# A gMLP block turned to have batch rows on lanes, and its output weight loaded as 72 lanes of 12 rows

## The chip, the core and the metric

The kernel runs on one core of a Trainium2 chip. The number that counts is the device time of one execution in microseconds (us). The kernel before takes 662.63 us, the median of three runs (662.47 to 662.69).

The core has five engines that matter here: TensorE (PE) multiplies, VectorE (DVE) and ScalarE (ACT) work on elements, GpSimd (POOL) sets up constants, and SyncE (SP) issues most of the transfers. Sixteen DMA engines carry data from HBM into SBUF, whose 128 partitions are called lanes below.

## The reference

One token for each of four batch rows goes through two branches that read the same normalised input, and their results are added to the input:

- x is 4 x 640; xn is its layer norm.
- Branch A is attention against a long cache: q = xn @ wq for 32 heads of 128; scores against 4096 cached keys for each row and head; softmax; the weighted sum of the cached values; then @ wo (4096 x 640). The two caches are 4 x 32 x 4096 x 128 in bf16 each, 134 MB each.
- Branch B is a gated MLP: z = gelu(xn @ w_in), with w_in 640 x 1728; z splits in two halves z1 and z2 of 864 columns; z2 is layer-normed over its 864 columns, multiplied by the single number w_sp and shifted by the single number b_sp; the product z1 * z2 goes through w_out (864 x 640).
- out = x + A + B.

Nearly all of the bytes are the caches: 282 MB are read in all, of which w_in is 2.2 MB and w_out 1.1 MB.

## The kernel before, in words

**Tiles.** The caches come in tiles of 128 lanes x 64 KB (8.4 MB): one tile holds one batch row's eight heads. There are 16 tiles of keys and 16 of values. Key tiles alternate between two buffers (the function `k_slot`); value tiles have a single buffer (`v_slot`). The two buffers of keys and the one of values are used for the weights first: `w_sb`, which sits in the buffer of the values, holds w_in (17,280 bytes in each lane) and behind it w_out; wq sits in one of the two key buffers.

**Order of the transfers.** SP issues all large transfers in the order of the program, and each of the 16 DMA engines takes its packets in that order: w_out's first part (L109), wq (L114), w_in (L121), w_out's rest (L123, four transfers), key tile 0 (L139, `load_k`), key tile 1 once wq has been read, value tile 0 (L145, `load_v`) once the gated MLP has read all of `w_sb`, key tile 2 once key tile 0 has been used up, and so on; wo comes last (L159, `load_wo`). A wait of SP for a buffer therefore stands in front of all transfers behind it.

**Order of the work.** The order on PE, DVE, ACT and SP is the program's (a manual schedule). After q, the first tile's query is spread over the lanes (`stage_q`), then comes `gmlp()`, then the loop over the tiles. For a tile, DVE multiplies keys by the query in two halves (L449), folds the product (L463), PE sums it (L475), DVE reduces the sums (L486) and the maxima, ACT takes the exponentials (L542), and PE weighs the values (L568). While tile i is multiplied, the values of tile i-1 are weighed. At the end wo's pieces are multiplied (`group_proj`, L216) as they land, and four small transfers write the result.

**The gated MLP before.** The 864 columns of a half lie as 128 x 6 and a rest of 96. Weights are the stationary side: for each half, seven groups of columns and five slices of the 640 inputs there is one matmul with 4 columns, the batch rows (L317, 70 in all), so that features lie on lanes and the four batch rows along them: 128 lanes x 56 numbers. The gelu (L326 to L337) runs on tiles of that size. The sums of the layer norm run across lanes, so they take a matmul with a column of ones (L342), a few instructions on one lane (L351 to L378), and a matmul with a row of ones that spreads the two resulting factors again (L387). The gated product `yT` has features on lanes already. Its rest of 96 features is turned by six small matmuls to 16 lanes of six rows (L408), and 12 groups of four matmuls (`add_out`, L216) add the product with w_out to `out_ps`.

**w_out before.** The first 768 rows go to 128 lanes with six rows, 7,680 bytes, each (L109). The last 96 rows go to lanes 0 to 15, six rows each, in four transfers of four lanes (L123); transfer l of them fills the lanes l, l+4, l+8 and l+12.

Of the kernel before, what the change touches and what calls it, by code (L numbers as in the profile page):

```python
# [17 lines left out]
def kernel(  # L18
# [35 lines left out]
    SLOT = NC * Dh  # L54
    CB = 4
    NB = NC // CB
    CG = 4
    GW = P // CG
# [5 lines left out]
    WJ = WH * Dh // P  # L64
    WW = 2
    WR = NG * ROWS
    NFF = Fh // P
    TL = 16
    TK = (Fh - NFF * P) // TL
    TE = 4  # L70
    NFC = NFF + TK
    F0 = NFF * P
    TF = TL * TK
    NZ = NFF + 1
    assert F0 + TF == Fh and TF <= P
    NQ = 4
    NO = D // NQ
    REP = GW // Bsz
# [5 lines left out]
    work = ctx.enter_context(tc.tile_pool(name="work", bufs=1))  # L84
# [12 lines left out]
    def v_slot(name):  # L97
# [7 lines left out]

    w_sb = v_slot("w_sb")
    w_in_sb = w_sb[:, 0 : DC * F].rearrange("p (c n) -> p c n", c=DC)
    w_out_sb = w_sb[:, DC * F : DC * F + NFC * D].rearrange("p (k n) -> p k n", k=NFC)
# [73 lines left out]
    for i in range(NSTAT):  # L182
# [9 lines left out]
        out=xn_bf,  # L192
# [21 lines left out]
    def add_out(lhsT, rhs, start=False, stop=False):  # L214
        for q in range(NQ):
            nc.tensor.matmul(  # L216
                out=out_ps[GW * q : GW * q + lhsT.shape[1], :],
                lhsT=lhsT,
                rhs=rhs[:, q * NO : (q + 1) * NO],
                start=start,  # L220
                stop=stop,
            )
# [36 lines left out]
    nc.gpsimd.tensor_copy(out=row_batch[:], in_=row_batch_f[:])  # L259


    HQ = 4
    NW = HQ * Dh
    q_rows = small.tile([P, 2, NW], BF16, tag="two_k", name="q_rows")
# [29 lines left out]
    load_k(1)  # L294


    GM = 2 * NZ * Bsz
    gm = {}
    gm_t = small.tile([P, 4 * GM + NZ * Bsz], FP32, tag="two_k", name="gm_t")
    for n, name in enumerate(("zz", "gw", "gt", "gz")):  # L300
        gm[name] = gm_t[:, n * GM : (n + 1) * GM].rearrange(
            "p (t k b) -> p t k b", t=2, b=Bsz
        )
    gm["sq"] = gm_t[:, 4 * GM :].rearrange("p (k b) -> p k b", b=Bsz)
    nc.gpsimd.memset(gm["zz"], 0.0)
    gm["st"] = work.tile([1, 5 * Bsz], FP32, name="st")
    gm["ac"] = work.tile([1, 2 * Bsz], FP32, name="ac")

    def gmlp():
        zz, gw, gt, gz, sq = (gm[n] for n in ("zz", "gw", "gt", "gz", "sq"))  # L310
        zT = ps_pv.tile([P, 2, NZ, Bsz], FP32, tag="pv", name="zT")
        for t in range(2):
            f1 = t * Fh + F0
            w_t = w_in_sb[:, :, t * Fh : f1].rearrange("p c (f k) -> p c k f", k=NFF)
            for k in range(NZ):
                for c in range(DC):
                    nc.tensor.matmul(  # L317
                        out=zT[: P if k < NFF else TF, t, k, :],
                        lhsT=w_t[:, c, k, :] if k < NFF else w_in_sb[:, c, f1 : f1 + TF],
                        rhs=xnT[:, c, :],  # L320
                        start=(c == 0),
                        stop=(c == DC - 1),
                    )
        nc.vector.tensor_copy(out=zz[:, :, 0:NFF, :], in_=zT[:, :, 0:NFF, :])
        nc.vector.tensor_copy(out=zz[:TF, :, NFF:NZ, :], in_=zT[:TF, :, NFF:NZ, :])
# [12 lines left out]
        nc.vector.tensor_tensor(out=sq, in0=gz[:, 1, :, :], in1=gz[:, 1, :, :], op=ALU.mult)  # L338

        s_ps = ps_m.tile([1, 2, NZ, Bsz], FP32, tag="m", name="ln_ps")  # L340
        for n, src in enumerate((gz[:, 1, :, :], sq)):
            nc.tensor.matmul(  # L342
                out=s_ps[:, n, :, :], lhsT=ones_col[:], rhs=src, start=True, stop=True
            )
        st, ac = gm["st"], gm["ac"]
        mean_t = st[:, 0:Bsz]
        ex2_t = st[:, Bsz : 2 * Bsz]
        var_t = st[:, 2 * Bsz : 3 * Bsz]
        rst_t = st[:, 3 * Bsz : 4 * Bsz]
        tmp_t = st[:, 4 * Bsz : 5 * Bsz]  # L350
        nc.vector.tensor_reduce(  # L351
            out=st[:, 0 : 2 * Bsz].rearrange("a (n b) -> a n b", b=Bsz),
            in_=s_ps[:].rearrange("a n k b -> a n b k"),
            axis=AX.X,
            op=ALU.add,
        )
        nc.vector.tensor_scalar(
            out=st[:, 0 : 2 * Bsz],
            in0=st[:, 0 : 2 * Bsz],
            scalar1=1.0 / float(Fh),  # L360
            scalar2=None,
            op0=ALU.mult,
        )
        nc.vector.tensor_tensor(out=tmp_t, in0=mean_t, in1=mean_t, op=ALU.mult)
        nc.vector.tensor_tensor(out=var_t, in0=ex2_t, in1=tmp_t, op=ALU.subtract)
        nc.scalar.activation(
            out=rst_t, in_=var_t, func=ACT.Sqrt, bias=eps_tile[:1], scale=1.0
        )
        wsp_t = work.tile([1, 1], FP32, name="wsp_t")
        nc.vector.tensor_copy(out=wsp_t[:], in_=wsp_bf[:])  # L370
        bsp_t = work.tile([1, 1], FP32, name="bsp_t")
        nc.vector.tensor_copy(out=bsp_t[:], in_=bsp_bf[:])
        nc.vector.reciprocal(out=rst_t, in_=rst_t)
        nc.vector.tensor_scalar(
            out=ac[:, 0:Bsz], in0=rst_t, scalar1=wsp_t[:, 0:1], scalar2=None, op0=ALU.mult
        )
        nc.vector.tensor_tensor(out=tmp_t, in0=ac[:, 0:Bsz], in1=mean_t, op=ALU.mult)
        nc.vector.tensor_scalar(  # L378
            out=ac[:, Bsz : 2 * Bsz],
            in0=tmp_t,  # L380
            scalar1=-1.0,
            scalar2=bsp_t[:, 0:1],
            op0=ALU.mult,
            op1=ALU.add,
        )
        ac_ps = ps_m.tile([P, 2 * Bsz], FP32, tag="m", name="ac_ps")
        nc.tensor.matmul(  # L387
            out=ac_ps[:], lhsT=ones_row[:], rhs=ac[:], start=True, stop=True
        )
        ac_sb = work.tile([P, 2 * Bsz], FP32, name="ac_sb")  # L390
        nc.scalar.copy(out=ac_sb[:], in_=ac_ps[:])
        nc.vector.tensor_tensor(
            out=sq,
            in0=gz[:, 1, :, :],
            in1=ac_sb[:, None, 0:Bsz].to_broadcast([P, NZ, Bsz]),
            op=ALU.mult,
        )
        nc.vector.tensor_tensor(
            out=sq,
            in0=sq,  # L400
            in1=ac_sb[:, None, Bsz : 2 * Bsz].to_broadcast([P, NZ, Bsz]),
            op=ALU.add,
        )
        yT = work.tile([P, NZ, Bsz], BF16, name="yT")
        nc.vector.tensor_tensor(out=yT[:], in0=gz[:, 0, :, :], in1=sq, op=ALU.mult)
        ye_ps = ps_m.tile([TL, TK, Bsz], FP32, tag="m", name="ye_ps")
        for k in range(TK):
            nc.tensor.matmul(  # L408
                out=ye_ps[:, k, :],
                lhsT=ident[:TF, :TF].rearrange("p (f k) -> p k f", k=TK)[:, k, :],  # L410
                rhs=yT[:TF, NFF, :],
                start=True,
                stop=True,
            )
        yE = work.tile([TL, TK, Bsz], BF16, name="yE")
        nc.scalar.copy(out=yE[:], in_=ye_ps[:])
        for k in range(NFC):
            if k < NFF:
                add_out(yT[:, k], w_out_sb[:, k, :])
            else:  # L420
                add_out(yE[:, k - NFF], w_out_sb[:TL, k, :])


    qbcs, scores, sums_ps, maxes, pms, pvs, es = {}, {}, {}, {}, {}, {}, {}
# [344 lines left out]
```

## Time and profile before

| what | value | where it is from |
|---|---|---|
| time, median of three runs | 662.63 us | timed runs |
| span of the profiled execution, first to last instruction | 661.1 us | page, head |
| around the span (start and end of the program) | 1.5 us | 662.63 less 661.1 |
| read from HBM | 282.24 MB, 427 GB/s over the span | page, part 3 |
| the large queue's share of the 16 DMA engines | 98.9% | page, part 3 |
| DVE busy | 491.6 us (74%) | page, part 1 |
| PE busy | 295.4 us (45%) | page, part 1 |
| gated MLP: first matmul to last | 23.85 to 35.64 us | timeline |
| DVE starts on key tile 0 | 43.24 us | timeline |
| last wo piece multiplied from | 657.27 us | timeline |

The page gives the profiled execution as one span, from its first instruction to its last, and that span is its own time; the timed runs are 1.5 us longer. In the views of transfers a window is cut into 40 slices, and a packet counts in the slice where it starts: one packet of 65,536 bytes in a slice of 0.1 us shows as 655 GB/s, one of 7,680 bytes as 77.

### The profile page before, as it was taken

The numbers are of one execution on the slowest core, as the hardware profiler recorded it, in microseconds if no ns is written. First come the engines' busy times: TensorE is split into PE (matmuls) and PEld (weight loads), VectorE is DVE, ScalarE is ACT, GpSimd is POOL, SyncE is SP. The second block draws the span as 40 slices with busy tenths as digits, with TensorE's granted clock in tenths as the row PEclk, the third lists the DMA queues.
The fourth block names the chain that finished last, engine by engine and source line by source line (L and its number), as shares of the span: only waits on it lengthen the run. The fifth ranks groups of instructions, "written<-read, shape, count | busy, mean of one in ns | idle before, by whom it ended". The sixth has DMA issues, their size and how long they took to land.

```text
span 661.1 us, 4720 instructions
## 1 busy us (share of the span) xinstructions
PE 295.4 (45%) x2099; PEld 127.9 (19%) x2099; DVE 491.6 (74%) x222; ACT 34.4 (5%) x94; POOL 2.1 (0%) x15
## 2 busy tenths in 40 slices
PE   0513464536426253552625344362634507263656
PEld 0301121212112021220202112120211202031223
DVE  1249999959597795959779569986959699695851
ACT  0300000000000000000000000000000000000000
POOL 1000000000000000000000000000000000000000
PEclk9756676876858687675868757787775768777688
DMA  8999999999999999999999999999999999999996
GB/s 377 456 428 444 428 417 441 429 436 441 436 420 433 432 429 445 440 421 432 424 436 441 440 425 432 420 441 436 437 428 437 425 432 429 440 432 437 432 406 275
DMA packets 5712, 282.55 MB, mean 427 GB/s; under 512 B 680, under 2 KB 812, under 8 KB 1084
## 3 DMA queue, kind: packets, MB, share of 16 engines
q1 hardware_dynamic: 5664, 282.24, 98.9%
q8 instruction: 16, 0.26, 0.2%
q14 instruction: 4, 0.03, 0.0%
q10 hardware_dynamic: 28, 0.01, 0.0%
HBM read 282.24 MB, written 0.01 MB: 427 GB/s over the span
## 4 chain that ended last, share of the span: by engine, by line
DMA 51%; DVE 37%; PE 9%; issue 2%; ACT 1%; SPq 0%; DVEq 0%; ACTq 0%
DMA k_nat<-in_A_k_cache_dram 47%; DVE k_nat L449 22%; DVE k_nat L463 11%; PE s_ps L475 8%; DMA wo<-in_A_wo_dram 4%; DVE s_sb L486 3%; DMA w_sb<-in_B_w_out_dram 1%; ACT p L542 1%; PE pv L568 1%; DVE m L495 1%; PE mT L500 0%; DVE nm L505 0%; DVE pm L553 0%; SPq L159 0%; PE out_ps L216 0%
## 5 line engine op out<-in xcount | busy, mean ns | idle before, releaser
L449 DVE TENSOR_TENSOR k_nat<-k_nat,qbc 128x16384 bf16<-128x16384 bf16 x32 | 278.0, 8688 | 97.8 <-DMA k_nat<-in_A_k_cache_dram 97.8
L475 PE MATMUL s_ps<-k_nat,ident 128*128 128x512 bf16 x528 | 184.8, 528 | 139.3 <-DVE k_nat L463 139.3
L463 DVE TENSOR_TENSOR k_nat<-k_nat 128x8192 bf16<-128x8192 bf16 x31 | 136.7, 4410 | 0.0
L475 PEld LDWEIGHTS <-ident 128*128 128x128 bf16 x528 | 65.3, 129 | 248.3 <-DVE k_nat L463 123.3
L500 PE MATMUL mT<-ident_f,m 128*1 128x128 f32 x16 | 5.9, 366 | 160.0 <-DVE m L495 160.0
L568 PE MATMUL pv<-v_nat,pm 128*32 128x512 bf16 x960 | 56.1, 387 | 0.8 <-DVE pm L553 0.8
L486 DVE TENSOR_REDUCE s_sb<-s_ps 128x128 f32<-128x1024 f32 x32 | 39.0, 1218 | 5.4 <-PE s_ps L475 5.4
L500 PEld LDWEIGHTS mT<-ident_f,m 128*1 128x1 f32 x16 | 1.3, 79 | 167.8 <-DVE m L495 156.2
L568 PEld LDWEIGHTS <-pm 128*32 128x32 bf16 x1024 | 27.1, 100 | 34.3 <-issue 8.5
L553 DVE TENSOR_TENSOR pm<-p,own_c 128x2048 bf16<-128x2048 bf16 x16 | 19.6, 1225 | 15.3 <-ACT p L542 15.3
L542 ACT ACTIVATE p<-s_sb,nb 128x256 bf16<-128x256 f32 x16 | 8.1, 508 | 394.1 <-DVE nb_h L524 394.1
L591 PE MATMUL o_ps<-e,pick 128*32 128x128 f32 x128 | 17.0, 276 | 11.2 <-ACT e L578 11.2
L591 PEld LDWEIGHTS o_ps<-e,pick 128*32 128x32 f32 x128 | 12.7, 109 | 18.7 <-ACT e L578 18.7
L578 ACT COPY e<-pv 128x512 f32<-128x512 f32 x16 | 9.4, 586 | 68.1 <-PE pv L568 60.6
L287 DVE COPY qT<-qT_ps 128x64 bf16<-128x64 bf16 x2 | 0.4, 224 | 15.5 <-PE qT_ps L282 15.5
L516 PE MATMUL nb_ps<-nm,ones_row 1*128 1x8 f32 x32 | 9.2, 359 | 6.0 <-DVE nm L505 6.0
L505 DVE TENSOR_REDUCE nm<-mT 1x8 f32<-1x128 f32 x16 | 4.5, 279 | 7.5 <-PE mT L500 7.5
L516 PEld LDWEIGHTS nb_ps<-nm,ones_row 1*128 1x128 f32 x32 | 7.7, 298 | 10.6 <-DVE nm L505 9.9
L271 PE MATMUL q_ps<-wq,xnT_r 128*32 128x512 bf16 x40 | 4.3, 609 | 11.2 <-DMA wq<-in_A_wq_dram 11.2
L443 ACT CAST qbc<-qbc_ps 128x128 bf16<-128x128 f32 x16 | 4.3, 266 | 92.3 <-PE qbc_ps L435 92.3
L608 PE MATMUL den<-ones_col,acc_h 128*32 128x1 f32 x8 | 1.0, 194 | 16.6 <-DVE acc_h L601 16.6
L495 DVE TENSOR_REDUCE m<-s_sb 128x1 f32<-128x256 f32 x16 | 6.7, 420 | 0.5
(92 smaller groups left out, 70.7 us busy)
## 6 DMA issues: line engine op xcount, KB each, us to landing
wq<-in_A_wq_dram SPq DMA_DIRECT2D x1, 5120.0 KB, 16.3
wo<-in_A_wo_dram SPq DMA_DIRECT2D x1, 2560.0 KB
w_sb<-in_B_w_in_dram SPq DMA_DIRECT2D x1, 2160.0 KB, 20.9
wo<-in_A_wo_dram SPq DMA_DIRECT2D x1, 1760.0 KB
w_sb<-in_B_w_out_dram SPq DMA_DIRECT2D x1, 960.0 KB
wo<-in_A_wo_dram SPq DMA_DIRECT2D x1, 640.0 KB, 25.5
k_nat<-in_A_k_cache_dram SPq DMA_DIRECT2D x16, 39.6
v_nat<-in_A_v_cache_dram SPq DMA_DIRECT2D x15, 33.7
```

The source lines that it names most:

```text
L449: nc.vector.tensor_tensor(out=part(i, u), in0=part(i, u), in1=qbcs[i][:, None, :].to_broadcast([P, UC, Dh]), op=ALU.mult,)
L463: nc.vector.tensor_tensor(out=t[:, :, 0:HD2], in0=t[:, :, 0:HD2], in1=t[:, :, HD2:Dh], op=ALU.add)
L475: nc.tensor.matmul(out=sums_ps[i][:, c : c + SC], lhsT=ident[:], rhs=t[:, c : c + SC, g * RW : (g + 1) * RW], start=(g == 0), stop=(g == n ...
L486: nc.vector.tensor_reduce(out=scores[i][:, u * UC : (u + 1) * UC], in_=sums_ps[i][:], axis=AX.X, op=ALU.add,)
L495: nc.vector.tensor_reduce(out=m1[:], in_=scores[i][:], axis=AX.X, op=ALU.max)
L500: nc.tensor.transpose(out=mT[:], in_=maxes[i][:], identity=ident_f[:])
L516: nc.tensor.matmul(out=nb_ps[:], lhsT=ones_row[:], rhs=maxes[i][:], start=True, stop=True)
L542: nc.scalar.activation(out=probs[i][:], in_=scores.pop(i)[:], func=ACT.Exp, bias=maxes.pop(i)[:], scale=scale_qk, accum_out=accs[hg][:, b ...
L553: nc.vector.tensor_tensor(out=pm[:], in0=probs.pop(i)[:] .rearrange("p (n c) -> p n c", c=CB)[:, :, None, :] .to_broadcast([P, NB, HT, CB] ...
L568: nc.tensor.matmul(out=pvs[i][j * GW : (j + 1) * GW, :], lhsT=pm[:, n, :, :].rearrange("p h c -> p (h c)"), rhs=v_nat[:, n * CB : (n + 1) ...
L578: nc.scalar.copy(out=es[i][:], in_=pvs.pop(i)[:].rearrange("p (c d) -> p c d", d=Dh))
L591: nc.tensor.matmul(out=o_ps[hg // NG][own_rows(hg), :], lhsT=pick[:, c, GW - HT - HT * b : 2 * GW - HT - HT * b], rhs=e[:, c, :], start=(b ...
```

## The change

The gated MLP is computed with the batch rows as the stationary side, and w_out is laid out anew.

- 20 matmuls of 32 x 432 (each of five input slices by four groups of lanes) replace the 70. The stationary side is xn with each batch row repeated eight times, as for q. Lanes 32j to 32j+31 hold the features of group j, three of every twelve columns; the result is 128 lanes x 432 numbers (both halves), every batch row eight times over.
- The gelu and the gate run on 128 x 432 and 128 x 216. The layer norm's sums run along a lane (two reductions) and then over the four groups with one matmul against a new constant, `same_row`, made of the identity matrix by one DVE reduction and one GpSimd copy. The factors then lie on every lane; the spreading matmul with its copy goes, and a small matmul spreads w_sp and b_sp.
- The gated product is turned by three transposes into 72 lanes, and 12 groups of `add_out` follow, with 72 lanes each.
- The working tiles and `same_row` now lie behind the weights in `w_sb`; a GpSimd memset and a tile of the small pool go.
- w_out goes to 72 lanes of 12 rows (15,360 bytes each): lanes 0 to 47 in one transfer ahead of wq, lanes 48 to 53, 54 to 59, 60 to 65 and 66 to 71 in four transfers behind w_in.

The number of transfers, their order and their 1,080 KB for w_out stay. Value tile 0 still goes into the buffer of `w_sb` when all of its readers are done.

```diff
+    FL = 72
+    FK = Fh // FL
+    FM = FK // CG
+    FC = Fh // CG
+    F_CUTS = (0, 48, 54, 60, 66, FL)
...
-    nc.sync.dma_start(
-        out=w_out_sb[:, 0:NFF, :], in_=B_w_out[0 : NFF * P].rearrange("(p k) n -> p k n", k=NFF)
-    )
+    w_out_sb = w_sb[:, DC * F : DC * F + FK * D]
+    spare = w_sb[:, DC * F + FK * D : SLOT].bitcast(FP32)
+    gm_sb = spare[:, 0 : 8 * FC]
+    same_row_f = spare[:, 8 * FC : 8 * FC + GW]
+    same_row = spare[:, 8 * FC + GW : 8 * FC + GW + P].rearrange("p (j r) -> p j r", j=CG)
+    w_out_v = B_w_out.rearrange("(p k) n -> p (k n)", k=FK)
+    nc.sync.dma_start(out=w_out_sb[: F_CUTS[1]], in_=w_out_v[: F_CUTS[1]])
...
     nc.sync.dma_start(out=w_in_sb, in_=B_w_in.rearrange("(p c) n -> p c n", c=DC))
-    for l in range(TL // TE):
-        nc.sync.dma_start(
-            out=w_out_sb[:TL, NFF:NFC, :].rearrange("(e l) k n -> e l (k n)", e=TE)[:, l],
-            in_=B_w_out[F0:Fh].rearrange("(e l k) n -> e l (k n)", e=TE, k=TK)[:, l],
-        )
+    for l0, l1 in zip(F_CUTS[1:], F_CUTS[2:]):
+        nc.sync.dma_start(out=w_out_sb[l0:l1], in_=w_out_v[l0:l1])
...
+    nc.vector.tensor_reduce(out=same_row_f, in_=ident_f[:].rearrange("p (j r) -> p r j", j=CG), axis=AX.X, op=ALU.add)
+    nc.gpsimd.tensor_copy(out=same_row, in_=same_row_f[:, None, :].to_broadcast([P, CG, GW]))
...
     def gmlp():
-        for t in range(2):
-            for k in range(NZ):
-                for c in range(DC):
-                    nc.tensor.matmul(
-                        out=zT[: P if k < NFF else TF, t, k, :],
-                        lhsT=w_t[:, c, k, :] if k < NFF else w_in_sb[:, c, f1 : f1 + TF],
-                        rhs=xnT[:, c, :],
...
+        z_ps = ps_pv.tile([P, 2, FC], FP32, tag="pv", name="z_ps")
+        w_v = w_in_sb.rearrange("p c (t l k) -> p c t l k", t=2, k=FK)
+        for c in range(DC):
+            for j in range(CG):
+                nc.tensor.matmul(
+                    out=z_ps[GW * j : GW * (j + 1), :, :],
+                    lhsT=xnT_r[:, c].rearrange("p b r -> p (b r)"),
+                    rhs=w_v[:, c, :, :, FM * j : FM * (j + 1)],
...
+        nc.vector.tensor_reduce(out=st[:, 0:1], in_=z2, axis=AX.X, op=ALU.add)
+        nc.vector.tensor_reduce(out=st[:, 1:2], in_=sq, axis=AX.X, op=ALU.add)
...
+        nc.tensor.matmul(out=s_ps[:, 0:2], lhsT=same_row.rearrange("p j r -> p (j r)"), rhs=st[:, 0:2], start=True, stop=True)
+        nc.tensor.matmul(out=s_ps[:, 2:4], lhsT=ones_row[:], rhs=wb[:], start=True, stop=True)
...
+        for m in range(FM):
+            nc.tensor.transpose(out=yT_ps[:, m].rearrange("p j b r -> p (j b r)"), in_=y_rows[:, :, m], identity=ident[:])
+        yT = work.tile([FL, FM, CG, Bsz], BF16, name="yT")
+        nc.scalar.copy(out=yT[:], in_=yT_ps[:, :, :, :, 0])
+        for k in range(FK):
+            j, m = divmod(k, FM)
+            add_out(yT[:, m, j, :], w_out_sb[:FL, k * D : (k + 1) * D])
```

More of the change, by code (lines that the diff above doesn't have):

```diff
@@ L66 @@
     WR = NG * ROWS
[L67 to L75, printed above, removed]
+    FL = 72
[3 more added lines that the diff above has]
+    F_CUTS = (0, 48, 54, 60, 66, FL)
+    assert FL * FK == Fh and FM * CG == FK
     NQ = 4
@@ L259 @@
     nc.gpsimd.tensor_copy(out=row_batch[:], in_=row_batch_f[:])
+    nc.vector.tensor_reduce(
+        out=same_row_f,
+        in_=ident_f[:].rearrange("p (j r) -> p r j", j=CG),
+        axis=AX.X,
+        op=ALU.add,
+    )
+    nc.gpsimd.tensor_copy(
+        out=same_row, in_=same_row_f[:, None, :].to_broadcast([P, CG, GW])
+    )
     HQ = 4
@@ L294 @@
     load_k(1)
[L297 to L307, printed above, removed]
[L309 to L325 removed]
+    def gmlp():
+        g_v = gm_sb.rearrange("p (w t f) -> p w t f", t=2, f=FC)
+        zz, gw, gt, gz = (g_v[:, n] for n in range(4))
+        z_ps = ps_pv.tile([P, 2, FC], FP32, tag="pv", name="z_ps")
[6 more added lines that the diff above has]
+                    rhs=w_v[:, c, :, :, FM * j : FM * (j + 1)],
+                    start=(c == 0),
+                    stop=(c == DC - 1),
+                )
+        nc.vector.tensor_copy(out=zz, in_=z_ps[:])
         nc.vector.tensor_tensor(out=gw, in0=zz, in1=zz, op=ALU.mult)
@@ L337, in gmlp @@
         nc.vector.tensor_tensor(out=gz, in0=zz, in1=gt, op=ALU.mult)
[L338 to L355, printed above, removed]
-        )
+        z1, z2 = gz[:, 0, :], gz[:, 1, :]
+        sq = gw[:, 0, :]
+        st = work.tile([P, 8], FP32, name="st")
+        nc.vector.tensor_tensor(out=sq, in0=z2, in1=z2, op=ALU.mult)
+        nc.vector.tensor_reduce(out=st[:, 0:1], in_=z2, axis=AX.X, op=ALU.add)
+        nc.vector.tensor_reduce(out=st[:, 1:2], in_=sq, axis=AX.X, op=ALU.add)
+        wb = work.tile([1, 2], FP32, name="wb")
+        nc.vector.tensor_copy(out=wb[:, 0:1], in_=wsp_bf[:])
+        nc.vector.tensor_copy(out=wb[:, 1:2], in_=bsp_bf[:])
+        s_ps = ps_m.tile([P, 4], FP32, tag="m", name="ln_ps")
+        nc.tensor.matmul(
+            out=s_ps[:, 0:2],
+            lhsT=same_row.rearrange("p j r -> p (j r)"),
+            rhs=st[:, 0:2],
+            start=True,
+            stop=True,
+        )
+        nc.tensor.matmul(
+            out=s_ps[:, 2:4], lhsT=ones_row[:], rhs=wb[:], start=True, stop=True
+        )
+        mean_t, ex2_t = st[:, 2:3], st[:, 3:4]
+        wsp_t, bsp_t = st[:, 4:5], st[:, 5:6]
+        var_t, rst_t = st[:, 6:7], st[:, 7:8]
         nc.vector.tensor_scalar(
-            out=st[:, 0 : 2 * Bsz],
-            in0=st[:, 0 : 2 * Bsz],
+            out=st[:, 2:4],
+            in0=s_ps[:, 0:2],
             scalar1=1.0 / float(Fh),
@@ L385, in gmlp @@
         )
-        ac_ps = ps_m.tile([P, 2 * Bsz], FP32, tag="m", name="ac_ps")
-        nc.tensor.matmul(
-            out=ac_ps[:], lhsT=ones_row[:], rhs=ac[:], start=True, stop=True
-        )
[L390 to L413, printed above, removed]
-            )
[L415 to L421, printed above, removed]
+        y_rows = small.tile([P, FL, FM], BF16, tag="two_k", name="y_rows")
+        nc.vector.tensor_tensor(
+            out=y_rows[:].rearrange("p l m -> p (l m)"), in0=z1, in1=sq, op=ALU.mult
+        )
+        yT_ps = ps_m.tile([FL, FM, CG, Bsz, REP], BF16, tag="m", name="yT_ps")
+        for m in range(FM):
+            nc.tensor.transpose(
+                out=yT_ps[:, m].rearrange("p j b r -> p (j b r)"),
+                in_=y_rows[:, :, m],
+                identity=ident[:],
+            )
+        yT = work.tile([FL, FM, CG, Bsz], BF16, name="yT")
[3 more added lines that the diff above has]
+            add_out(yT[:, m, j, :], w_out_sb[:FL, k * D : (k + 1) * D])
     qbcs, scores, sums_ps, maxes, pms, pvs, es = {}, {}, {}, {}, {}, {}, {}
```

28 lines of the change are left out of this document (12 added, 16 removed).

## The prediction

> **What bounds the kernel now.** First the page's shares and queues, then the chain that ended last, then the timeline around the gated MLP, then the transfers in two short windows. From the page:
>
> ```profile
> span 661.1 us, 4720 instructions
> ...
> DMA  8999999999999999999999999999999999999996
> ...
> q1 hardware_dynamic: 5664, 282.24, 98.9%
> q8 instruction: 16, 0.26, 0.2%
> ...
> DMA 51%; DVE 37%; PE 9%; issue 2%; ACT 1%; SPq 0%; DVEq 0%; ACTq 0%
> ```
>
> The DMA engines are never idle for long: 282 MB at their rate is the time. A step matters only if it adds work to the engine that ends last, or leaves engines without a queued transfer. The chain's first 120 us:
>
> ```profile
> 0.73 4.59 DMA w_sb<-in_B_w_out_dram
> ...
> 5.96 37.25 DMA k_nat<-in_A_k_cache_dram
> 43.21 0.02 issue
> 43.24 8.70 DVE k_nat L449
> ...
> 70.46 8.60 DVE k_nat L449
> ```
>
> From the landing of key tile 0 on, DVE works without a pause. The gated MLP is not in the chain. The timeline shows why:
>
> ```profile
> 23.85 3.73 PE L317 MATMUL zT<-xnT_r,w_sb 128*128 128x4 bf16 x70 [0.88 <-DMA w_sb<-in_B_w_out_dram]
> ...
> 34.68 0.96 PE L216 MATMUL out_ps<-w_sb,yE 16*4 16x160 bf16 x24
> 35.70 0.33 SPq L145 DMA_DIRECT2D v_nat<-in_A_v_cache_dram  x1
> 43.24 8.69 DVE L449 TENSOR_TENSOR k_nat<-k_nat,qbc 128x16384 bf16<-128x16384 bf16 x1 [9.67 <-DMA k_nat<-in_A_k_cache_dram]
> ...
> 76.89 0.33 SPq L139 DMA_DIRECT2D k_nat<-in_A_k_cache_dram  x1
> ```
>
> DVE stood idle 9.67 us before key tile 0. Value tile 0, issued at 35.70, queues behind key tile 1, whose packets last until 60.5 (43.24 less 2, plus eight packets of 2.42 us): 25 us to spare. Key tile 2, issued at 76.89, has only 2.9 us: the trace's packets show the first engines start it at 79.8, two engines late, at 80.6.
>
> Transfers from 20.5 to 24.5 us, 40 slices of 0.1 us, a packet counted where it starts:
>
> ```profile
> DMA  8999804999900999911311311509900000000999
> GB/s 346 864 518 691 346 0 173 518 864 691 518 0 0 1311 3277 2622 886 77 77 154 77 77 154 77 77 231 0 655 1966 0 0 0 0 0 0 0 0 1311 3277 1966
> ```
>
> From 21.8 on twelve packets of key tile 0 start (1311, 3277, 2622 and one in 886), while four engines first work through L123's: one packet of 7,680 B is 77. Four rounds of four follow; the four then start the tile at 23.2 (655 and 1966). So the four transfers of four lanes all went to the same four engines, one lane each, 0.29 us a packet, and these run 1.2 to 1.4 us behind. They stay behind, because each engine's queue is never empty, and key tile 0 lands with the last of them.
>
> **The change, part by part.**
>
> *Matmuls and element work.* 70 matmuls (3.73 us) become 20 of 432 columns. q's 40 of 512 columns took 4.26 us at a granted clock of 1.00, 107 ns each: 2.1 us, or 4.3 at 0.50. Their operand comes in runs of three numbers; L475 reads runs of eight and shows 425 ns from one matmul to the next at half clock, so no extra is charged. Six operations on 128x432 replace six on 128x56: from 0.19 us for 56 elements and 1.22 us for the 1024 of L486 some 1.1 ns an element, 0.6 each, 3.6 us; five on 216 at 0.37, 1.9 us; tanh as L578's 128x512, 0.6; eight small ones at 0.15 to 0.22, 1.4; the two small matmuls 0.4, square root and gaps 1.0, three transposes and their copy 0.8. 48 matmuls of `add_out` stay at 1.9. Together 16 us instead of 11.8: `gmlp` ends near 40 instead of 35.6, its DVE work near 37. Cost on the path: nothing. Cover: DVE's idle time to 43.24, and 25 us at SP. Beyond them each us would be paid.
>
> *Constants.* A DVE reduction (0.3, as L228) and a POOL copy (0.3) run near 7 us, when DVE waits for wq until 22 and POOL has nothing more. The memset goes. Nothing.
>
> *SP.* As many issues in the same order. The last of L123 still waits for w_out's first part (5.3 us before; up to 2.5 later), and key tile 0 behind it: hidden, since wq and w_in occupy the engines until 21.8.
>
> *w_out's first part.* 128 lanes of 7,680 B, eight packets per engine at 0.29: 2.3 us. Now 48 lanes of 15,360 B, three per engine. No row has this length; w_in's 17,280 B took 0.64 (27 B/ns), so 0.57 each, 1.7 us, if every lane takes data at its engine's full rate. No row shows fewer than 128 lanes filled by 16 engines. All rows give an engine 27 B/ns whatever the packet's length; that can be the engine's limit or that of 16 ways into SBUF, eight lanes each. In the latter case L123, with lanes four apart at full rate, allows a way at most four neighbouring lanes. The other four lie elsewhere, perhaps also among the 48; then a way has eight packets to take, 4.6 us. Ends: -0.6 and +2.3.
>
> *w_out's rest.* Four transfers of four lanes (four packets, 1.17 us on four engines) become four of six neighbouring lanes, on six engines by the same rule. Lower end: each lane at full rate, 4 x 0.57 = 2.3, +1.1. Upper end: neighbouring lanes 48-51, 52-55, ... share a way. Engines 0 to 3 need 4 x 0.57 = 2.3 in the first transfer and 2.3 in the third (60-63); in the second (54, 55 / 56-59) and fourth (66, 67 / 68-71) engines 2 and 3 need 1.15 to 2.3. Sum 6.9 to 9.2; the higher, where these ways are also used by key tile 0 on the engines that go on. +5.7 to +8.0.
>
> I choose sharing, near its upper end: +2.2 and +7.3. One row is nearest to full rate (L123), but it is the one whose lanes lie four apart; the only row with neighbouring lanes, x's four packets of 1,280 B within 0.11 us, is 5 KB in all and could sit in a buffer, whereas each shared group here is 61 KB.
>
> [...]
>
> *What follows.* Key tile 0 lands 9.5 us later, DVE starts at 52.7, and key tile 2 is issued at 86.4. Its 2.9 us of room are gone, two engines had none: they start it 9.5 late. The engines that carried the extra packets are late by 9.5 in their own queues, with no idle time later that would absorb it. At the end engines finish wo between 653.3 and 657.1; those last got two instruction packets (q8) each, about 1.5 us apiece by the gap and the slower packet behind it. The most delayed of the four L123 engines were some 0.4 ahead of them, so +9.1 to +9.5 arrives. The last lines stay as they are, 4 us later than the last packet:
>
> ```profile
> 657.27 0.64 PE L216 MATMUL out_ps<-wo,oT 128*4 128x160 bf16 x20 [0.62 <-DMA wo<-in_A_wo_dram]
> ```
>
> Sum: span 661.1 + 9.3 = 670.4; 1.5 us lie around the span (662.63 less 661.1): 671.9, taken as 672.
>
> **Rivals.**
>
> 1. *Lanes don't share* (not slower, the other side): the engine sets the rate. -0.6 + 1.1 = +0.5 on six engines, -0.6 on ten. Key tile 0 lands 0.5 later, and so does key tile 2's issue: 663.1, within the 0.2% (1.3 us) that a measurement of this kernel can tell from no change. For it: x's packets, the row above. It decides if a six-lane transfer's packets take 0.57.
> 2. *Sharing by neighbours alone*: the first part costs nothing (12 groups of four lanes, 4 x 0.57 = 2.3, as before), the rest 5.7: 668.3; with less than full sharing down to 665.
> 3. *Faster*: the six-lane transfers move on to other engines each time, all work evens out: -0.6 + 24 x 0.57 / 16 = +0.3 against 1.2 on the late engines: -0.9 at key tile 0, 661.8; a larger gain has no source. Against it: four times the same four engines.
> 4. *Full sharing in the worst order* (engines take lanes e, e+16, e+32, so that every engine waits in the first part, 6.9 instead of 2.3): +4.6 and +7, 674.2.
> 5. *`gmlp` outlasts its cover*: with operands at a quarter of the rate, 20 matmuls take up to 17 us; without sharing DVE starts 6 late, 668; with sharing it stays hidden.
>
> **How the numbers follow.** Sharing with pairs (670 to 673.5) 0.50; rival 4 and beyond 0.08; rival 2 with its partial forms 0.20; rival 1 0.16; rival 3 0.03; rival 5 0.03. Range: from rival 1's 663.0 to 674.5; what lies outside is some 0.1, and without rival 1 the low end would leave out over 0.2. The likeliest case alone spans 670 to 673.5. Faster by over 0.2%: 0.02; within: 0.17; slower: 0.81.
>
> **What would show it.** Right: in the window after w_in, six engines' 15,360 B packets last 1.1 to 2.3 us instead of 0.57; wq lands up to 2.5 later (17.5 before); DVE starts key tile 0 near 52.7 with more idle time before it, key tile 2 is issued near 86, and the DMA digits dip around 80 to 90. `gmlp` ends near 40 and its DVE work stays ahead of key tile 0. Wrong: packets of 0.57 us, and DVE at 43.7; or a `gmlp` that DVE is still in when key tile 0 lands.

## The result and the profile after

The changed kernel takes 673.03 us (median of four runs, 671.35 to 674.07) against 662.58 for the kernel before on the same chip (662.47 to 662.69): a ratio of 1.0153, 95% interval 1.0141 to 1.0165. The profiled execution is the shortest of the four, 671.35 us with a span of 669.5, which is 8.4 us over the 661.1 of the kernel before. From its page:

```profile
span 669.5 us, 4608 instructions
...
DMA  9999999999999999999999999999999999999996
GB/s 299 319 436 435 439 439 436 431 424 431 432 431 431 439 428 435 439 436 435 428 431 432 435 439 428 435 432 427 435 439 436 435 431 428 431 436 431 435 410 263
...
DMA 52%; DVE 36%; PE 9%; issue 2%; ACT 1%; SPq 0%; DVEq 0%; ACTq 0%
```

The kernel before has this line in its page:

```profile
GB/s 377 456 428 444 428 417 441 429 436 441 436 420 433 432 429 445 440 421 432 424 436 441 440 425 432 420 441 436 437 428 437 425 432 429 440 432 437 432 406 275
```

The DMA engines are at least as busy as before in all slices, but in the first two (0 to 33 us) they move 299 and 319 GB/s instead of 377 and 456. A slice is 16.7 us, so (377 + 456) x 16.5 less (299 + 319) x 16.7 is 3.4 MB that is still to be moved at 33 us; at 430 GB/s that is 8 us. From the third slice on both run alike. The whole loss lies in the first 33 us, in transfers that are busy and slow. The chain of the changed kernel, its start:

```profile
0.74 7.71 DMA w_sb<-in_B_w_out_dram
...
8.77 43.32 DMA k_nat<-in_A_k_cache_dram
...
52.11 8.70 DVE k_nat L423
```

Key tile 0 ends at 52.11 instead of 43.24. The timeline around the gated MLP and behind it:

```profile
20.43 3.76 PE L278 MATMUL q_ps<-wq,xnT_r 128*32 128x512 bf16 x40 [13.50 <-DMA wq<-in_A_wq_dram]
...
25.75 2.11 PE L311 MATMUL z_ps<-w_sb,xnT_r 128*32 128x432 bf16 x20 [0.35 <-DMA w_sb<-in_B_w_in_dram]
...
37.51 1.77 PE L213 MATMUL out_ps<-w_sb,yT 72*4 72x160 bf16 x48 [0.28 <-ACT yT L392]
...
39.43 0.33 SPq L142 DMA_DIRECT2D v_nat<-in_A_v_cache_dram  x1
...
52.11 8.69 DVE L423 TENSOR_TENSOR k_nat<-k_nat,qbc 128x16384 bf16<-128x16384 bf16 x1 [15.48 <-DMA k_nat<-in_A_k_cache_dram]
...
85.70 0.33 SPq L136 DMA_DIRECT2D k_nat<-in_A_k_cache_dram  x1
```

q's matmuls start at 20.43 instead of 17.51, so 2.9 us are lost before w_in. The gated MLP is over at 39.3, and DVE then stands idle for 15.48 us instead of 9.67: more room than before, not less. The transfers from 20.5 to 34.5, in 40 slices of 0.35 us, where a packet counts in the slice in which it starts:

```profile
DMA  5939594989999096005533093309959950004899
GB/s 247 642 148 642 247 642 197 592 346 494 538 661 1574 0 176 88 0 0 88 88 44 44 0 275 44 44 0 231 749 187 749 749 187 0 0 0 187 374 1498 562
```

A packet of 64 KB counts 187 here and one of 15,360 B 44. Ten engines start key tile 0 together (661 and 1574, near 24.6). Then come the packets of the four six-lane transfers, one or two in a slice, to 31 us. The ten engines' next packets start only at 30 to 32 (749, 187, 749, 749). In the trace's packet records the first packets of these ten engines last 5.5 to 6.5 us and their second ones 2.7 to 3.7; from then on nearly all last 2.42, as in the kernel before. Of the 24 packets of 15,360 B in these four transfers the first seven last 0.57 to 1.04 us, the other seventeen 1.49 to 2.06.

### The profile page after: what moved, and what is told of

The parts are those of the page before. It is cut to its first block, busy times and chain, and to the rows that moved or that the text cites. A ratio compares the mean times of both kernels' runs of the same rounds, so it can differ in the third digit from the quotient of the medians.

```text
span 669.5 us, 4608 instructions
## 1 busy us (share of the span) xinstructions
PE 293.5 (44%) x2044; PEld 125.6 (19%) x2044; DVE 494.4 (74%) x223; ACT 34.6 (5%) x93; POOL 2.3 (0%) x15
## 4 chain that ended last, share of the span: by engine, by line
DMA 52%; DVE 36%; PE 9%; issue 2%; ACT 1%; SPq 0%; DVEq 0%; ACTq 0%
DMA k_nat<-in_A_k_cache_dram 47%; DVE k_nat L423 22%; DVE k_nat L437 10%; PE s_ps L449 8%; DMA wo<-in_A_wo_dram 4%; DVE s_sb L460 3%; DMA w_sb<-in_B_w_out_dram 1%; ACT p L516 1%; PE pv L542 1%; DVE m L469 1%; PE mT L474 0%; DVE nm L479 0%; DVE pm L527 0%; SPq L156 0%; PE out_ps L213 0%
## 5 line engine op out<-in xcount | busy, mean ns | idle before, releaser
L278 PE MATMUL q_ps<-wq,xnT_r 128*32 128x512 bf16 x40 | 3.8, 547 | 13.5 <-DMA wq<-in_A_wq_dram 13.5
L542 PE MATMUL pv<-v_last,pm 128*32 128x512 bf16 x64 | 5.8, 542 | 4.3 <-DMA v_last<-in_A_v_cache_dram 4.3
```

The lines of the kernel that those rows point to most:

```text
L542: nc.tensor.matmul(out=pvs[i][j * GW : (j + 1) * GW, :], lhsT=pm[:, n, :, :].rearrange("p h c -> p (h c)"), rhs=v_nat[:, n * CB : (n + 1) ...
```

## The experiments

The theory, as in the prediction: lanes that share a way into SBUF delay the engines that write them, and the DMA time so lost moves everything behind it. The traces show when a packet starts, how long it lasts and its size; which lane it writes, which engine writes which lane and what a way is are in none of them. The rivals: the late key tile is what costs, not the DMA time; the new gMLP costs time of its own; small transfers are dear, whatever their lanes; or the addresses read in HBM matter, not the lanes written.

### The transfers moved behind key tile 0

Two runs move w_out's transfers behind key tile 0's. The first moves the four six-lane ones:

```
     nc.sync.dma_start(out=w_in_sb, ...)
-    for l0, l1 in zip(F_CUTS[1:], F_CUTS[2:]):
-        nc.sync.dma_start(out=w_out_sb[l0:l1], in_=w_out_v[l0:l1])
...
     load_k(0)
+    for l0, l1 in zip(F_CUTS[1:], F_CUTS[2:]):
+        nc.sync.dma_start(out=w_out_sb[l0:l1], in_=w_out_v[l0:l1])
```

> The changed kernel, with the four six-lane transfers of w_out queued behind key tile 0 instead of ahead of it. Sharing (neighbouring lanes of one transfer share a way into SBUF, so DMA time is lost for good): key tile 0 lands only some 2 us late, DVE starts near 45.5 us instead of 52.1, but the transfers take their 7 to 8 us out of the key and value tiles behind them: total 669 to 673 us. Late tile (the cost is only that key tile 0 lands late): total 664 to 665. Own work of the new gated MLP: still 671 to 674, with DVE busy where it waits now.

The second moves all five, the 48 lanes too.

> The changed kernel with all of w_out (the 48 lanes and the four six-lane transfers) queued behind key tile 0. Late tile: key tile 0 lands at 40 us, and the total is that of the kernel before or less, 661.5 to 662.7 us. Sharing: the lost DMA time stays, now in the packets of key tile 1 and value tile 0: 668 to 672.

Measured: 672.7 us (ratio 1.0146, 1.0131 to 1.0161) and 672.27 (1.0146). With all five behind, DVE starts key tile 0 even earlier than in the kernel before, and the hole in the page's rates moves to the third slice:

```profile
GB/s 372 448 238 423 438 431 434 434 431 422 419 438 438 438 427 434 434 431 438 435 434 435 438 426 431 430 435 434 434 422 435 438 434 439 434 427 434 430 413 248
...
42.80 8.69 DVE L424 TENSOR_TENSOR k_nat<-k_nat,qbc 128x16384 bf16<-128x16384 bf16 x1 [9.99 <-DMA k_nat<-in_A_k_cache_dram]
```

So the transfers cost the same 10 us wherever they stand. A late start of DVE is not needed for it; the DMA time is lost either way.

### The kernel before with its transfers moved

The same move was made in the kernel before, whose transfers of w_out are cheap:

```
-    nc.sync.dma_start(out=w_out_sb[:, 0:NFF, :], ...)
...
-    for l in range(TL // TE):
-        nc.sync.dma_start(out=w_out_sb[:TL, NFF:NFC, :]...[:, l], ...)
...
     load_k(0)
+    (both, unchanged)
```

> The kernel before with all of w_out's transfers issued behind key tile 0 instead of ahead of wq and behind w_in; nothing else is changed. If the position of w_out costs the kernel before nothing but a later key tile 0: VectorE starts key tile 0 some 2 to 4 us earlier, the DMA engines move the same bytes at the same rate, and the total is 662.1 to 662.7. If an earlier start of VectorE is worth time (the rival): below 661. If the position matters for the changed kernel alone, because there the transfers are slow, this run stays at 662.6 as its two counterparts stayed at 672.

It took 670.36 us (1.0118, 1.0103 to 1.0133), outside what either theory gave. Its packets have their usual lengths (0.29, 0.64, 1.51 and 2.42 us), but for some of wq's very first, single ones beside instruction packets, and the sixteen that start after the idle time shown below (2.75 to 3.38). The timeline shows why it is slow, and the second fence shows the transfers from 67 to 101, in slices of 0.85 us:

```profile
43.57 3.73 PE L316 MATMUL zT<-xnT_r,w_sb 128*128 128x4 bf16 x70 [21.59 <-DMA w_sb<-in_B_w_out_dram]
...
53.21 8.68 DVE L448 TENSOR_TENSOR k_nat<-k_nat,qbc 128x16384 bf16<-128x16384 bf16 x1
```

```profile
DMA  3997998899589830000000009203908909909519
GB/s 154 694 463 308 463 463 386 386 463 617 231 386 694 386 154 0 0 0 0 0 0 0 0 0 1157 77 0 154 1079 0 386 848 0 713 540 0 925 231 77 1157
```

The matmuls on w_in wait for w_out, though they don't read it: w_in and w_out lie in one tile, and the program orders a transfer whose lanes lie four apart as if it also wrote what lies beside them. In the two runs above, with neighbouring lanes, the matmuls on w_in did not wait (they start at 26.05 and 21.92). So the whole gMLP came after 43 us, and DVE reached key tile 0 at 53.21, 10 us late. The slot of key tile 0 was released late too, and no packet of 64 KB starts from 79.2 to 87.7 (the zeros); the last ones end between 79.9 and 81.6, so the engines had no work for 6 to 8 us. This is another way to lose nearly the same time, without slow packets of w_out.

### Lanes or addresses

In the kernel before, the four small transfers of the remainder write lanes four apart from rows four apart. One run makes only the lanes neighbours, the other only the rows:

```
-            out=w_out_sb[:TL, NFF:NFC, :].rearrange("(e l) k n -> e l (k n)", e=TE)[:, l],
+            out=w_out_sb[TE * l : TE * (l + 1), NFF:NFC, :].rearrange("e k n -> e (k n)"),
```

> The kernel before, and in its four transfers of four lanes each only the lanes are changed: transfer l fills lanes 4l to 4l+3 in place of lanes l, l+4, l+8 and l+12. The rows that it reads lie four apart as before, so the remainder's rows land on other lanes and the output is that of a permuted w_out. The theory (a lane whose way belongs to another engine is what costs): the four engines write through one way, packets of 7,680 B go from 0.29 us to 1.1 to 1.2, the four engines lag by 4.6 us in place of 1.2, and other engines' first packets of key tile 0 are stretched beyond 2.42; the total rises by 2 to 6 us, to 664.5 to 668.5. The rival (the addresses read in HBM decide): packets 0.29 us and 662.6.

```
-            in_=B_w_out[F0:Fh].rearrange("(e l k) n -> e l (k n)", e=TE, k=TK)[:, l],
+            in_=B_w_out[F0:Fh].rearrange("(l e k) n -> l e (k n)", e=TE, k=TK)[l],
```

> The kernel before, and in its four transfers of four lanes each only the source is changed: the lanes lie four apart as before, and the four rows that one transfer reads are neighbours in HBM. Rows land on other lanes, so the output is that of a permuted w_out. The theory (lanes decide): packets of 7,680 B at 0.29 us, key tile 0's at 2.42, total 662.3 to 662.9, as before. The rival (the addresses read in HBM decide, neighbouring rows being slow): packets of 1.1 us or more and 664.5 to 668.5.

Neighbouring lanes: 663.66 us (1.0016, 1.0006 to 1.0026). Neighbouring rows: 662.69 (1.0002, 0.9992 to 1.0011). So the lanes matter and the addresses don't. But the effect is 1 us, below the 2 to 6 expected: the packets last 0.46 us in the mean and 0.79 at most, not 1.1. Transfers from 21 to 29, slices of 0.2 us (a packet of 64 KB counts 328), with neighbouring lanes:

```profile
DMA  0992999721060930900099000007009799000097
GB/s 0 432 864 86 983 2371 732 154 38 38 0 154 0 655 77 0 655 0 0 0 2294 1638 0 0 0 0 0 328 0 0 655 328 2048 1638 0 0 0 0 328 328
```

and in the kernel before:

```profile
DMA  2990991221290000990000097000990000097000
GB/s 86 691 605 0 2294 1754 77 115 115 77 115 1311 0 0 0 0 2294 1638 0 0 0 0 0 983 328 0 0 0 1966 1966 0 0 0 0 0 983 328 0 0 0
```

Twelve engines start key tile 0 at 21.8. In the kernel before their second packets start 2.4 us later (2294, 1638 at 24.2), here 3.2 us later (25.0), although these twelve had nothing to do with the remainder. These 0.8 us on engines that carry none of it are about the size of the whole effect. Why it is so small stays open: the first four packets, on four neighbouring lanes at once, still took 0.29 us each, so the sharing is not simply one rate divided among the lanes.

### Lanes four apart, three runs that waited

Three runs write w_out in the changed kernel by transfers whose lanes lie four apart. One does so for the rest alone:

```
-    for l0, l1 in zip(F_CUTS[1:], F_CUTS[2:]):
-        nc.sync.dma_start(out=w_out_sb[l0:l1], in_=w_out_v[l0:l1])
+    for l in range(4):
+        nc.sync.dma_start(out=apart(w_out_sb)[:, l], in_=apart(w_out_v)[:, l])
```

where `apart(t)[:, l]` are lanes 48 + l, 52 + l, and so on to 68 + l.

> As the run with the rest behind key tile 0, and each of the four transfers takes six lanes that lie four apart (48, 52, ... 68 and so on), the same rows on the same lanes. Sharing: the packets of these transfers take 0.57 us instead of 1.5 to 2, and of the loss only the first part's remains: 664 to 666.5 us. Six engines' load without sharing, or the new gated MLP's own work: no difference to the run with neighbouring lanes.

One does so for all: lanes 0 to 31 in four transfers of eight, 32 to 71 in four of ten.

> The changed kernel with all of w_out in transfers of lanes four apart: lanes 0 to 31 in four transfers of eight ahead of wq, lanes 32 to 71 in four of ten behind key tile 0. Sharing: no packet is slowed, DVE starts key tile 0 near 42 us, and the total is 662 to 663.5, the kernel before within a fifth of a per cent. Own work of the gated MLP, or 72 lanes as such: still 668 or more.

A third has the second part in half rows behind key tile 0:

> The changed kernel with w_out filled lane by lane in another order: lanes 0 to 31 in four transfers of eight lanes that lie four apart, ahead of wq, and lanes 32 to 71 in eight transfers of ten lanes four apart, half a row each, behind key tile 0. The 72 lanes of 12 rows and the new gMLP are as in the changed kernel. The theory (what the change loses is DMA time, lost because its engines write lanes whose way into SBUF belongs to another engine; with lanes four apart, as the run with all of w_out apart showed, each engine keeps to its own way): packets of 0.57 us for a whole row and 0.29 for half a row, key tile 0's packets at 2.42 again, VectorE starts key tile 0 near 42 to 44, and the total is 662.0 to 663.5, the whole loss undone. A first rival (the new gMLP or its later end costs time of its own, which the two runs with lanes apart hid behind a wait for w_out): 665 or more, with VectorE late at key tile 0. A second (small transfers cost DMA time each, whatever their lanes): twelve transfers in place of five, so 673 or more.

They took 677.93, 676.77 and 676.7 us (1.0235, 1.0207 and 1.0211), all slower than the changed kernel, and all for the reason just seen, here in the second:

```profile
47.82 2.13 PE L315 MATMUL z_ps<-w_sb,xnT_r 128*32 128x432 bf16 x20 [21.26 <-DMA w_sb<-in_B_w_out_dram]
...
58.63 8.69 DVE L427 TENSOR_TENSOR k_nat<-k_nat,qbc 128x16384 bf16<-128x16384 bf16 x1
```

The gMLP started behind key tile 0, and the 10.8 us from its first matmul to DVE's start on key tile 0 were paid in full. The third run's time fits both of its rivals, but this wait, not the gMLP's own work, put it there. In the third run SP's eight transfers also kept key tile 1 back, which it issued at 46.11 instead of 29.13 as in the second, and engines stood idle for some 5 us before it. The times say nothing about lanes; the packets do. With lanes 32 to 71 in four transfers of ten behind key tile 0, a packet of 15,360 B lasts 0.57 us and the packets of 64 KB beside it 2.42. With lanes 48 to 71 in four transfers of six, the packets last 1.15 to 1.2 after the first ones (0.63 to 0.79), and the ten other engines' packets of 64 KB 4.3 to 4.75.

### The same without the wait

To be rid of that wait, w_in was put into the free end of wq's slot, so that w_out lies in a slot of its own. A control has this alone:

```
-    w_in_sb = w_sb[:, 0 : DC * F]...
-    wq_t = k_slot("wq")[:, 0 : DC * HD]...
+    wq_slot = k_slot("wq")
+    wq_t = wq_slot[:, 0 : DC * HD]...
+    w_in_sb = wq_slot[:, DC * HD : DC * (HD + F)]...
```

> A control for the next two runs. The changed kernel, with w_in put into the free end of wq's slot instead of w_out's slot; the DMA order, the 72 lanes and the transfers of w_out are as in the changed kernel. The point: a transfer with lanes four apart no longer counts as overlapping w_in, so in the next two runs the gMLP's matmuls need not wait for w_out. By every theory this control itself stays where the changed kernel is: VectorE starts key tile 0 near 52, 671 to 674.

671.39 us (1.0129, 1.0113 to 1.0144), DVE at 52.60: the changed kernel, as expected. On top of it, the first part stays one transfer of 48 neighbouring lanes, now 24 to 71, and the rest, lanes 0 to 23, goes out behind w_in in four transfers of six lanes that lie four apart:

```
-    nc.sync.dma_start(out=w_out_sb[: F_CUTS[1]], in_=w_out_v[: F_CUTS[1]])
+    nc.sync.dma_start(out=w_out_sb[24:FL], in_=w_out_v[24:FL])
...
-    for l0, l1 in zip(F_CUTS[1:], F_CUTS[2:]):
-        nc.sync.dma_start(out=w_out_sb[l0:l1], in_=w_out_v[l0:l1])
+    for l in range(4):
+        nc.sync.dma_start(out=w_out_sb[l:24:4], in_=w_out_v[l:24:4])
```

> [...] The prediction had the first part at +2.2 us and the rest, by neighbouring lanes, at +7.3. If that split is right and neighbouring lanes are what makes the rest dear: wq's last packets end 2.2 to 2.9 us later than before (19 to 19.8), the rest's packets take 0.57 us and cost the slowest engines 4 x 0.57 - 1.17 = 1.1 us, key tile 0's packets take 2.42 from the first, VectorE starts key tile 0 at 46 to 47.5, and the time is 665 to 667. If the four small transfers are dear by themselves, or the first part carries most of the loss: VectorE at 50 or later and 669 or more.

666.9 us (1.0066, 1.0053 to 1.008). The transfers from 24 to 32 in slices of 0.2 us, first the control, then this run, then this run's chain:

```profile
DMA  6999995950660050950606500950050900999999
GB/s 259 778 587 732 1541 1137 77 154 77 0 77 77 0 0 77 0 154 77 0 77 0 77 77 0 0 154 77 0 0 77 0 732 0 0 1311 328 983 328 983 655
```

```profile
DMA  9993333351399990000000077999000000077999
GB/s 481 2043 1214 154 154 154 154 154 230 77 154 481 655 2621 1638 0 0 0 0 0 0 0 0 328 328 2949 655 983 0 0 0 0 0 0 0 328 328 2949 655 983
```

```profile
0.74 7.26 DMA w_sb<-in_B_w_out_dram
...
8.72 38.03 DMA k_nat<-in_A_k_cache_dram
...
46.77 8.70 DVE k_nat L424
```

Both start ten engines on key tile 0 in the first 1.2 us. In the control the four transfers trickle on for 7.3 us, from 24.7 to 32.0 (one 77 in a slice is one packet), and the ten engines' second packets wait until 30.2. Here the rest is through in 2.9 us, from 24.0 to 26.9, and the ten go on at 26.6 and 29.0, one packet in 2.42 us. The two kernels issue as many transfers of as many bytes in the same order; only the lanes differ, and this is 5.8 us at key tile 0 (52.60 to 46.77) and 4.5 us of the time. Not all of it is the rest's: the 48 lanes are others too (24 to 71 for 0 to 47), and w_in's last packets end 0.5 us earlier than in the control (24.0 to 24.6 for 24.5 to 25.1), so 5.3 us are left for the rest. Small transfers as such are not the cause.

Then all of w_out by lanes four apart, in eight transfers: 0 to 31 in four of eight ahead of wq, 32 to 71 in four of ten behind w_in:

```
-    nc.sync.dma_start(out=w_out_sb[: F_CUTS[1]], in_=w_out_v[: F_CUTS[1]])
+    for l in range(4):
+        nc.sync.dma_start(out=w_out_sb[l:32:4], in_=w_out_v[l:32:4])
...
-    for l0, l1 in zip(F_CUTS[1:], F_CUTS[2:]):
-        nc.sync.dma_start(out=w_out_sb[l0:l1], in_=w_out_v[l0:l1])
+    for l in range(32, 36):
+        nc.sync.dma_start(out=w_out_sb[l:FL:4], in_=w_out_v[l:FL:4])
```

> [...] The 72 lanes of 12 rows and the new gMLP stay. The theory (the loss is DMA time lost by writing lanes that belong to another engine): packets of 15,360 B at 0.57 us, key tile 0's at 2.42 from the first, the eight engines that carry w_out have 8 packets of 0.57 = 4.6 us where the kernel before has 8 of 0.29 and, on four engines, 4 more = 3.5 us, so the slowest is 1.1 us later: VectorE starts key tile 0 at 44 to 45.5 and the time is 663 to 665. The rival (the new gMLP, its DVE operations or its later end cost time of their own, or eight engines carrying w_out is itself what costs): VectorE after 48 and 667 or more.

666.88 us (1.0063, 1.005 to 1.0075), DVE at 47.82: between what the two gave, and no better than with the 48 neighbouring lanes kept. Behind w_in all is as the theory has it: 0.57 us a packet, 2.42 for key tile 0. What was missed lies in the first 8 us. The four transfers of eight lanes start most of their packets one after the other (near 2.3, 3.2, 3.9 to 4.1, 4.6 to 5.1), a packet takes 0.6 to 1.1 us, and the engines start wq between 4.77 and 7.50, where the kernel before starts it between 4.62 and 5.00 and the changed kernel between 4.71 and 7.24. Part of it is SP: it needs 2.85 us to issue the four transfers, 0.7 us for each, so an engine's packets cannot follow one another at 0.57, and wq is issued behind them at 3.63 instead of 1.20:

```profile
0.73 2.85 SPq L111 DMA_DIRECT2D w_sb<-in_B_w_out_dram  x4
3.63 0.45 SPq L116 DMA_DIRECT2D wq<-in_A_wq_dram  x1
```

The last engine to start key tile 0 does so at 28.09, not at 23.39: 2.5 us from the start of wq, 1.1 us from the four further packets (4 x 0.57 less 1.17), some 1 us not accounted for.

### The rest moved on by four lanes

Last, the same kernel with the rest moved on by four lanes: lanes 36 to 71 go out in four transfers of nine lanes behind w_in, and 32 to 35 one by one ahead of it:

```
+    for l in range(32, 36):
+        nc.sync.dma_start(out=w_out_sb[l : l + 1], in_=w_out_v[l : l + 1])
     nc.sync.dma_start(out=w_in_sb, ...)
-    for l in range(32, 36):
+    for l in range(36, 40):
         nc.sync.dma_start(out=w_out_sb[l:FL:4], in_=w_out_v[l:FL:4])
```

> [...] If what costs is two engines on one way: packets of 0.57 us but for the last one or two engines, key tile 0's first packets stretched on two engines at most, and 663.5 to 666. If what costs is an engine on a way that is not its own: all nine engines' packets above 0.8 us, the first packets of key tile 0 stretched on all engines to 3.5 us or more, VectorE at 47 or later, and 667 to 671.

670.32 us (668.61 to 672.74; 1.0116, 1.0095 to 1.0137), DVE at 50.74. Of the two answers the time is the second's, the packets are nearer to the first's. Part of the time has another cause: SP issued key tile 0 only at 21.43, and the first engines through with w_in, from 22.58 on, found no packet of it before 23.16 to 24.5, some 9 us of engine time in all. Until 24.8 nearly all packets of 15,360 B behind w_in last 0.57 us, a few 1.0 to 1.2. From 24.8 on they take 0.6 to 1.25, and key tile 0's that are under way 3.2 to 4.7. So the packets up to 24.8 speak against the second answer, and key tile 0's are stretched as it had it; whose lanes an engine wrote, and what ended the 0.57 us, is not shown.

## Why the prediction was right where it was

The forecast was 672.0, and the time is 673.03. So close a match is in part luck: the terms add up to a loss of 9.3 us, the profiled execution lost 8.4, and what puts the median 1.7 us above the profiled execution is in no trace. The steps, with what the runs say of each:

- *Sharing among neighbouring lanes*: that the lanes decide is shown. Six-lane transfers with neighbouring lanes against six-lane transfers with lanes four apart are worth 4.5 us of the time (671.39 to 666.9; of the 5.8 us at key tile 0 some 0.5 belong to the first part), and in the kernel before a change of lanes alone is felt while a change of addresses is not. How the lanes share is argued from the lengths of packets; the ways by which the terms +2.2 and +7.3 were worked out are in no trace. In place of the two terms the runs show +2.4 to +2.8 and +6.1.
- *w_out's first part, +2.2*: wq's last packets end at 19.1 to 19.9 instead of 16.7 to 17.1, so +2.4 to +2.8: a little under-sized. The 48 lanes take from 1.7 to 7.2 us, 5.5 where the prediction's upper end had 4.6.
- *w_out's rest, +7.3*: over-sized by about 1 us. DVE starts key tile 0 8.9 us later, of which 2.8 are there at the end of w_in (25.0 for 22.2), so 6.1 are left; the least of it, +1.1, and the 5.3 us between the control and the run with the rest on lanes four apart make 6.4. The reason is right only in part. The prediction let six engines fall behind and kept the ten others free, and expected the DMA digits to dip at 80 to 90. They stay at 9: the ten engines' own packets were stretched from 2.42 to 5.5 to 6.5 us, so that all sixteen were late when key tile 2 was issued, and there was no idle time to show. Their four packets took the six engines 4.5 to 6.9 us, where 6.9 to 9.2 was forecast for the slowest. The dip that it described is real, but belongs to other cases: the kernel before with its transfers moved, where DVE alone is late, and the run with all on lanes four apart behind w_in, where five engines stood idle for some 2 us from 80.9 on.
- *What follows: key tile 0 late, then key tile 2, then the end*: DVE at 52.11 (forecast 52.7), issue of key tile 2 at 85.70 (86.4), span +8.4 (+9.3). The room before key tile 2 was read too wide: in the kernel before with moved transfers its packets start 1.0 to 1.6 us after its issue (87.7 to 88.4 for 86.75), and that comes off the 2.9 us; one engine, not two, waited for it in the kernel before (79.84 to 80.58). Wherever the loss lies ahead of key tile 0 or in DVE's start, the span follows that start:

| run | DVE starts key tile 0 | span |
|---|---|---|
| kernel before | 43.24 | 661.1 |
| neighbouring rows, neighbouring lanes | 43.55, 44.65 | 660.8, 662.1 |
| rest on lanes four apart, all on lanes four apart, gMLP not waiting | 46.77, 47.82 | 665.1, 665.8 |
| shifted by four lanes | 50.74 | 668.5 |
| changed kernel, control | 52.11, 52.60 | 669.5, 670.2 |
| kernel before with transfers moved | 53.21 | 669.5 |
| lanes four apart, gMLP waiting | 58.63, 59.01, 60.32 | 674.5, 674.7, 675.9 |

The two runs with slow transfers behind key tile 0 are off this line (45.42 and 42.80, with 671.0 and 670.7), since they lose the DMA time after that point.

- *gMLP, constants and SP cost nothing on the path*: shown by DVE's 15.48 us of idle time before key tile 0, and by the same line, on which kernels with the old and the new gMLP lie together. The gMLP ends at 39.3 (forecast 40), but two errors cancel in that: it began 1.9 us later (25.75 for 23.85) and took 13.5 us, not 16. The 16 counted 4.3 us for the 20 matmuls, at half the clock; they took 2.11, at a granted clock of 1.00. What is shown too is that the cover is needed: where the gMLP began behind key tile 0, its 10.8 us were paid.
- *Rival 1, lanes don't share*, fell, though not with the first packets: seven of the 24 took 0.57 to 1.04 us, the others 1.49 or more. *Rival 2, neighbours alone*, named the larger part but not the first part's loss. *Rival 4* stayed out of reach of the median; the two longest runs, 674.03 and 674.07, came near its 674.2, but neither has a trace.

No version that was run beats the kernel before. What stays open: why transfers to neighbouring lanes stretch packets of engines that carry none of them, which lanes share, and why the changed kernel's runs spread over 2.7 us while the control's spread over 0.7.

## What to carry to other kernels

When a matrix is spread over fewer than 128 lanes, look at which lanes one transfer fills at the same moment: here lanes four apart, from lane 0 or 32 on, kept a packet behind w_in or key tile 0 at 0.57 us for 15,360 B, while from lane 48 on it lasted 1.15 to 1.2 after the first ones; neighbouring lanes made it 1.6 times (0.46 us for 0.29 in the mean) to 3.6 times (2.06 for 0.57 at most) as long and slowed other transfers with it. Busy DMA digits hid the loss (9 in the changed kernel's first two slices, at 299 and 319 GB/s for 377 and 456); the rate per slice and the length of a packet of known size show it. And before moving or splitting a transfer, see which waits its tile gives to others, and what it holds up in the issuing queue: four runs here were slow through a wait that no data needed, and in two a tile was issued late behind small transfers (46.11 us for 29.13, 21.43 for 8.63).

## What the hardware showed that was not expected

- Transfers to neighbouring lanes slowed engines that carried none of them. Key tile 0's first packets went from 2.42 us to 5.5 to 6.5 in the changed kernel, on all ten engines alike, and to 3.1 to 3.2 in the kernel before with neighbouring lanes, where four engines carried the remainder and the twelve others nothing of it. With all of w_out behind key tile 0, 64 KB packets took up to 7.65.
- Lanes four apart were not all alike. With lanes 0 to 23 or 32 to 71 behind w_in, a packet of 15,360 B lasted 0.57 us and one of 64 KB beside it 2.42 throughout; with 48 to 71 they lasted 1.15 to 1.2, after the first ones, and 4.3 to 4.75; with 36 to 71 behind w_in 0.57 at first, from 24.8 us on 0.6 to 1.25, and 3.2 to 4.7.
- At the start of the program four transfers of eight lanes deliver their packets no faster than one transfer of 48 neighbouring lanes: the last engine starts wq at 7.50 against 7.24. Their issue alone takes SP 2.85 us.
- Some kernels with stretched packets differ from run to run: 671.35 to 674.07 for the changed kernel and 668.61 to 672.74 with the shift, against 662.47 to 662.69 for the kernel before and 666.66 to 667.06 with the rest on lanes four apart. It is no rule: the control, with stretched packets, has 671.24 to 671.94, and the run with all lanes four apart and the gMLP waiting 674.81 to 677.44.
